# Last section of a Fourier convolution: TensorE in place of VectorE turns the blocks of the inverse, and the convolution's order is ranked anew

## The chip, the cores and the metric

The kernel runs on one core of a Trainium2 chip. The metric is the device time of one execution in microseconds (us), lower is better: the median of three runs is given, and the profile comes from one execution taken by the hardware profiler. Engines are named as in the profile: PE is TensorE (matmuls and turns), DVE is VectorE, ACT is ScalarE, POOL is GpSimd, SP issues most of the DMAs.

## The reference

One block of a sequence model on x of 2048 positions (L) by 512 channels (D), fp32. First a long convolution (a state-space kernel K made from 128 modes for each channel, applied by FFT of length 2L), then a mixer with two matmul layers and shifts along the sequence, then a two-layer MLP.

```
x = A_u
xn = layernorm(x)
K[d, l] = 2 Re sum_n C[d,n] dt[d] exp((-exp(log_A_real) + i A_imag)[d,n] dt[d] l)
y = irfft(rfft(xn, 2L) * rfft(K, 2L))[:L] + xn * D_skip
h = x + y
b = layernorm(h)
hs = shift(gelu(layernorm(b) @ w1)) @ w2      # quarters of the channels shifted by +1, -1, +2, -2
x1 = b + hs
out = h + x1 + gelu(layernorm(x1) @ w3) @ w4  # w3: 512 x 1792
```

## The kernel before

**The convolution** (`conv_phase`) works on four sections of 128 channels, numbered 0 to 3. The transform of 2048 positions is split into a part of 32 (stage A, small tables `fas`, `fis`) and a part of 64 (stage B, tables `tbs`, `ms`). The tile `h` holds the sequence as 128 partitions by 16 tiles by 512 channels. For each section:

- tables of cosines and sines in chunks of 16 channels (`table`: tiles `pt`, `cs`, `sn`, `amx`, `amp`, `E`), which ACT, DVE and POOL make together, and PE sums them to the taps `kt` (`taps`);
- stage A of the taps and of x, whose results DVE turns in blocks of 32 by 32 into `at` (`stage_a_turn`, `stage_a_x`; `stage_a_taps` for the parts that ACT copies);
- eight products e = 0 to 7 (`product`): stage B by PE (`bank<-at,tbs`), a complex product by DVE or POOL into a tile u (the names `u`, `thp`, `ini` rotate as its four homes), in part with two sums;
- the inverse of stage B (`stage_b_inv`, `bank<-u,ms`), whose 8 results ACT or DVE evict into `at`;
- DVE turns `at` in four pieces (`turn_inv`, STREAM_TRANSPOSE), and PE runs the inverse of stage A with `fis`; the result is added to `h` (`stage_a_inv`; for section 3 `last_a_inv`).

In section 3 `last_a_inv` first lays the four quarters of `h` (q = 3, 0, 1, 2: tiles 4q to 4q+3) into four banks with identity matmuls (`keep`), adds 64 small inverse matmuls to them, and ACT copies the four banks back into `h`. From the bank of q = 3 DVE also takes the statistics of tiles 12 to 15 (`part`), then means (`mvh`), and a root with one step on ACT (`ra`, `rb`, `rr`, `rn`).

**The mixer** (`mixer_phase`) begins with these tiles: `norm1(3)` normalizes tiles 12 to 15 on DVE into the first `xq` tile, `turn1(3)` turns them with 16 PE transposes into the banks `xt` (four blocks for each of the two first tiles, then the rest), ACT casts them to a high part `xt3ch` and DVE subtracts for the low part `xt3cl`, and `layer1(3, 0)` starts (`l<-xt30h,...`). From there on, matmuls of the layers follow each other to the end; the other quarters are normalized beside them.

**What sets the order.** In the convolution every step is handed to a planner (`Plan.add`) with its engine, a cost, and what it reads and writes. The planner plays the steps against these costs; where several are ready at about the same time, the table `RANK` decides. The result is one fixed order for each engine, and each engine executes its order strictly. `SHARE` says which of two engines does a shareable step. Where the planner sees PE idle it adds filler matmuls of the identity (`busy`, `bank<-ident`). In the mixer the program text is the order. PSUM has 8 banks: in the convolution two double banks (called 94 and 95 in the orders below), two single ones (96, 97), and a double one for `amx`; the mixer's `xt` banks take the space of 96, 97 and `amx`, and its other banks that of 94 and 95.

Of the kernel before, what the change touches and what calls it, by code (L numbers as in the profile page):

```python
# [1986 lines left out]
```

## Time and profile before

| what | value |
|---|---|
| median of 3 runs | 679.01 us (678.62 to 680.68) |
| profiled execution | 678.03 us |
| its span, first to last instruction | 675.8 us |
| mean granted clock of TensorE | 0.992 |
| TensorE busy | 640.8 us (95%) |
| VectorE busy | 574.7 us (85%) |
| ScalarE, GpSimd busy | 403.7 us, 398.9 us |
| start of the first layer-1 matmul | 299.83 us |

A busy TensorE includes the filler matmuls. The convolution is what runs before 299.83, the mixer what runs after it. A row of the timeline gives start, length, engine, line of the source, operation, output and inputs by name, shapes, how many instructions are merged, and, in brackets, how long the engine was idle before and who ended that. Nearly all instructions bear the line of a recording helper, so tiles tell them apart, not lines.

### The profile page before, as it was taken

The numbers are of one execution on the slowest core, as the hardware profiler recorded it, in microseconds if no ns is written. First come the engines' busy times: TensorE is split into PE (matmuls) and PEld (weight loads), VectorE is DVE, ScalarE is ACT, GpSimd is POOL, SyncE is SP. The second block draws the span as 40 slices with busy tenths as digits, with TensorE's granted clock in tenths as the row PEclk, the third lists the DMA queues.
The fourth block names the chain that finished last, engine by engine and source line by source line (L and its number), as shares of the span: only waits on it lengthen the run. The fifth ranks groups of instructions, "written<-read, shape, count | busy, mean of one in ns | idle before, by whom it ended". The sixth has DMA issues, their size and how long they took to land.

```text
span 675.8 us, 17748 instructions
## 1 busy us (share of the span) xinstructions
PE 640.8 (95%) x7232; PEld 509.2 (75%) x7232; DVE 574.7 (85%) x992; ACT 403.7 (60%) x700; POOL 398.9 (59%) x411
## 2 busy tenths in 40 slices
PE   2959999999999999999999999999999999999997
PEld 2946666773677584768888888888888889999986
DVE  5999998999899999889978799866688678888896
ACT  7998877888798883245534555544465344435430
POOL 1959798899888798502677209355511634456340
PEclk9998998999999999999999999999999999999999
DMA  8944632000301133020262524455664355434104
GB/s 201 293 134 121 206 120 48 17 3 3 81 2 50 48 114 95 2 63 1 64 202 52 167 79 156 156 179 157 195 218 140 103 162 184 129 110 141 32 0 125
DMA packets 52149, 73.58 MB, mean 109 GB/s; under 512 B 7396, under 2 KB 27108, under 8 KB 52068
## 3 DMA queue, kind: packets, MB, share of 16 engines
q1 hardware_dynamic: 50308, 69.82, 34.2%
q10 hardware_dynamic: 1248, 1.57, 0.9%
q0 software_dynamic: 512, 1.05, 0.7%
q8 instruction: 57, 0.93, 0.6%
q14 instruction: 24, 0.20, 0.1%
HBM read 44.90 MB, written 21.23 MB: 98 GB/s over the span
## 4 chain that ended last, share of the span: by engine, by line
PE 61%; DVE 4%; ACT 1%; issue 1%; DVEq 0%; ACTq 0%
PE l L140 20%; PE acc L140 7%; PE bank L140 6%; PE l3d L140 3%; PE l3a L140 3%; PE l3g L140 3%; PE l3f L140 3%; PE l3e L140 3%; PE l3c L140 3%; PE l3b L140 3%; PE res L140 2%; DVE u L140 1%; DVE at L140 1%; PE l4y L140 1%; PE l4x L140 1%; PE l4z L140 1%
## 5 line engine op out<-in xcount | busy, mean ns | idle before, releaser
L140 POOL TENSOR_TENSOR pt<-p,s 128x512 int32<-128x512 int32 x64 | 70.8, 1118 | 8.9 <-DVE sn L140 8.4
L140 ACT ACTIVATE pt<-pt 128x1056 f32<-128x1056 int32 x64 | 69.8, 1097 | 6.7 <-DVE cs L140 3.6
L140 PE MATMUL bank<-at,tbs 128*64 128x128 f32 (+1 forms) x768 | 65.5, 315 | 3.7 <-issue 1.1
L140 PEld LDWEIGHTS bank<-at,tbs 128*64 128x64 f32 x768 | 45.4, 135 | 20.3 <-issue 2.7
L140 PE MATMUL bank<-u,ms 64*128 64x128 f32 x736 | 47.6, 279 | 0.5 <-DVE u L140 0.5
L140 PEld LDWEIGHTS bank<-u,ms 64*128 64x128 f32 x736 | 43.0, 188 | 5.7 <-issue 2.0
L140 PEld LDWEIGHTS bank<-ident 128*128 128x128 f32 x310 | 37.1, 195 | 13.1 <-issue 5.3
L140 DVE TENSOR_TENSOR cs<-pt,amx 128x512 f32<-128x512 f32 x64 | 41.5, 677 | 2.1 <-ACT pt L140 1.5
L140 PE MATMUL bank<-ident 128*128 128x128 f32 x310 | 41.1, 285 | 0.7 <-DVE at L140 0.7
L140 POOL TENSOR_TENSOR cs<-pt,amp 128x512 f32<-128x512 f32 x26 | 32.5, 1252 | 9.4 <-ACT pt L140 5.4
L140 ACT ACTIVATE pt<-pt,halfpi 128x1056 f32<-128x1056 f32 x32 | 38.0, 1187 | 0.1
L140 ACT COPY at<-bank 128x512 f32<-128x512 f32 x37 | 23.1, 628 | 22.2 <-PE bank L140 22.0
L140 POOL TENSOR_TENSOR sn<-pt,amp 128x512 f32<-128x512 f32 x28 | 34.0, 1216 | 3.7 <-issue 2.0
L140 PE MATMUL bank<-cs 128*32 128x64 f32 x1024 | 32.5, 224 | 3.1 <-DVE cs L140 2.2
L140 DVE STREAM_TRANSPOSE at<-bank 128x512 f32<-128x512 f32 (+1 forms) x36 | 33.3, 953 | 1.4 <-PE bank L140 1.4
L140 PEld LDWEIGHTS bank<-cs 128*32 128x32 f32 x1024 | 23.7, 111 | 13.8 <-issue 4.6
L140 PE MATMUL bank<-sn 128*32 128x64 f32 x1024 | 31.8, 221 | 0.6 <-issue 0.5
L140 DVE TENSOR_TENSOR u<-xs,bank 128x1024 f32<-128x1024 f32 x23 | 27.9, 1217 | 3.1 <-ACT xs L140 2.7
L140 DVE TENSOR_TENSOR amx<-E,amx 128x512 f32<-128x512 f32 (+1 forms) x32 | 26.5, 829 | 3.4 <-ACT amx L140 3.3
L140 PE MATMUL bank<-h,fas 32*32 32x512 f32 x256 | 22.9, 755 | 6.8 <-ACT h L140 5.8
L140 POOL TENSOR_TENSOR cs0w<-raw,cs0w 128x512 fp32r<-128x512 f32 x5 | 6.5, 1299 | 36.7 <-ACT cs0w L140 25.5
L140 POOL TENSOR_TENSOR amp<-E,ec 128x512 f32<-128x512 f32 x23 | 24.5, 1072 | 4.1 <-DVE E L140 2.7
(1278 smaller groups left out, 2157.3 us busy)
## 6 DMA issues: line engine op xcount, KB each, us to landing
raw<-in_B_w_dram SPq DMA_DIRECT2D x28, 256.0 KB, 2.9
xq<-xq SPq DMA_DIRECT2D x72, 64.0 KB, 2.0
h<-in_A_u_dram SPq DMA_DIRECT2D x32, 128.0 KB, 4.2
h<-in_A_u_dram SPq DMA_DIRECT2D x16, 256.0 KB, 4.3
kept<-ptw SPq DMA_DIRECT2D x8, 512.0 KB, 4.4
ms<-in_mm_dram SPq DMA_DIRECT2D x4, 768.0 KB, 6.5
ptw<-kept SPq DMA_DIRECT2D x6, 512.0 KB, 4.9
out_dram<-h SPq DMA_DIRECT2D x46, 64.0 KB, 1.7
```

The lines of the kernel that those rows point to most:

```text
L140: ins = f(*args, **kw)
```

## The change

1. In section 3 (`PET = (3,)`) the inverse of stage B exchanges its operands: u is the stationary one, the table `ms` the moving one. The result comes out with channels on partitions. Its eviction into `at` writes four neighbours in a row (`128x128x4`), reading the bank with neighbours 128 or 512 elements apart; before, it read and wrote pairs.
2. The four VectorE transposes of section 3 go. Instead `turn_pe` turns eight groups of four 128 x 128 blocks on PE into a bank, and each is evicted (seven by ACT, one by DVE: `tev`). The inverse of stage A then reads its moving operand in order, with 16 matmuls of 512 columns instead of 64 of 128.
3. `last_a_back` keeps only q = 3 in a bank (one identity matmul instead of four). q = 0 and q = 2 are added to `h` by DVE; q = 1 is copied out by ACT (into the first part of `ms`) and added by POOL (`TAIL`).
4. The four normalizations of tiles 12 to 15 are planned in the convolution, write to the u tiles, which are now one tile `uu` that is also the first `xq` tile of the mixer, and the bias `rn` of the other quarters is worked out ahead of them, not behind.
5. `RANK` is new (1260 steps instead of 1252), and `SHARE` too. What VectorE does more or less by it: 2 steps of `E` fewer, 1 `amp` fewer, 1 `cs` and 2 `sn` more, 1 copy of `kt` more, 2 evictions of the far spectra (`sxv`) fewer and 1 of the near ones (`xsv`) more; the product of (section 2, e = 6) goes to POOL and that of (3, 4) comes back; of the inverse evictions (`ibv`, 7 as before) three instead of two are in section 3; of the sums section 3 has two on DVE instead of three, section 2 one as before. ACT and POOL get the rest.

Of the diff, the tables `SHARE` and `RANK` are cut:

```diff
--- before.py
+++ after.py
@@ -20,7 +20,7 @@
 EPS = 1e-5
 WID = (128, 128, 128, 128)
 CH = 16
...
 
 
 XS = 2
@@ -33,61 +33,63 @@
 LOOK = 0.05
 BS = (0, 1, 2, 3)
 FILL0 = 8.0
+PET = (3,)
+TAIL = ('dve', 'pool', 'dve')
 FILLC, FILLN = 0.3, 128
 RANK = (
-    143, 142, 183, 178, 179, 198, 203, 195, 202, 194, 189, 200, 208, 231, 207, 233, 220, 219, 196, 199, 223, 221, 225, 227,
...
+    343, 327, 391, 392, 390, 404, 399, 398, 407, 405, 402, 397, 430, 427, 456, 426, 410, 412, 403, 409, 428, 448, 436, 431,
...
 )
 TURN = 2.0 ** 32
 TWO_PI = 2.0 * math.pi
...
@@ -856,7 +860,9 @@
-    uu = [tile(f"u{i}", [128, 8 * W]) for i in range(2)]
+    cst["uu"] = tp.tile([128, 16 * W], F32, tag="uu", name="uu")
+    cst["home"] = lambda name: tp.tile([128, 16 * W], F32R, tag="uu", name=name)
+    uu = [cst["uu"][:, i * 8 * W : i * 8 * W + 8 * W] for i in range(2)]
     xs = [tile(f"xs{i}", [128, 4 * W]) for i in range(XS)]
     g_ = [t.rearrange("p (d i t) -> p d i t", i=32, t=2) for t in uu]
     uu += [t.rearrange("p g i d -> p (g i d)") for t in (thp, ini)]
@@ -985,13 +991,92 @@
                 for i, (m, t) in enumerate(terms):
                     for par in range(2):
                         f = slice(par * 64, par * 64 + 64)
+                        if s in PET:
+                            pe.matmul(plan.view(p)[:, par, pair * 128 : pair * 128 + 128], q[f, t, pair, :],
+                                      ms[f, m, e * 2 + pair, :],
+                                      start=(i == 0), stop=(i == len(terms) - 1))
+                            continue
                         pe.matmul(plan.view(p)[:, par, pair * w_ : pair * w_ + w_], ms[f, m, e * 2 + pair, :], q[f, t, pair, :],
                                   start=(i == 0), stop=(i == len(terms) - 1))
 
         p = add("PE", 0.02 + len(terms) * w_ * 4.0e-3, mm, dense=0.83, r=uk + [("mm", e // 2), ("su", s, e, 0), ("su", s, e, 1)], w=keys, bank=2)
-        dst = whole(s, 0).rearrange("p (d k t) -> p k d t", k=32, t=2)[:, e * 4 : e * 4 + 4].rearrange("p (a b) d t -> p a b d t", a=2)
-        evac("ibv", (s, e), n, 0.22 + n * 0.51e-3, dst,
-             lambda: plan.view(p)[:, :, 0 : 2 * w_].rearrange("p a (b d t) -> p a b d t", b=2, t=2), w=keys, frees=p)
+        if s in PET:
+            dst = at[:, 0].rearrange("p (i x e k) -> p e i x k", x=4, e=8, k=4)[:, e]
+            src = lambda: plan.view(p)[:, :, 0:256].rearrange("p a (b x i) -> p i x a b", b=2, x=4)
+        else:
+            dst = whole(s, 0).rearrange("p (d k t) -> p k d t", k=32, t=2)[:, e * 4 : e * 4 + 4].rearrange("p (a b) d t -> p a b d t", a=2)
+            src = lambda: plan.view(p)[:, :, 0 : 2 * w_].rearrange("p a (b d t) -> p a b d t", b=2, t=2)
+        evac("ibv", (s, e), n, 0.22 + n * 0.51e-3, dst, src, w=keys, frees=p)
+
+    def turn_pe(s, n, g, gk):
+
+        def tr():
+            for m in range(4):
+                i = n * 4 + m
+                pe.transpose(plan.view(p)[:, m * 128 : m * 128 + 128], at[:, 0, i * 128 : i * 128 + 128], ident)
+
+        p = add("PE", 0.43, tr, dense=0.0, r=[("a0", e, n) for e in RE], bank=1, w=gk)
+        evac("tev", (s, n), 512, 0.48, g, lambda: plan.view(p)[:, 0:512], w=gk, frees=p)
+
+    def stage_a_back(s, q):
+        hv = h[:, q * 4 : q * 4 + 4, OFF[s] : OFF[s + 1]]
+        u = uu[q % 2].rearrange("p (i n) -> p i n", i=2)
+        hadd = OFF[s] // 64 + q // 2 in SHARE["hadd"]
+        for i in range(2):
+            turn_pe(s, i * 4 + q, u[:, i], [("u", q % 2, i)])
+
+        def mm():
+            b = plan.view(p)
+            if hadd:
+                pe.matmul(b, ident, hv, start=True, stop=False)
+            for c in (0, 2, 1, 3):
+                pe.matmul(b[quarter(c)], fis[:, c // 2, :], u[:, c % 2], start=not hadd, stop=True)
+
+        p = add("PE", 2.24 if hadd else 1.12, mm, dense=0.76, r=[("u", q % 2, i) for i in range(2)] + ["fis", ("h", s, q)], bank=1)
+        if hadd:
+            add("ACT", 0.5, lambda: act.copy(hv, plan.view(p).rearrange("p (j d) -> p j d", j=4)), w=[("h", s, q)], frees=p)
+        else:
+            add("DVE", 0.6, lambda: v.tensor_tensor(hv, hv, plan.view(p).rearrange("p (j d) -> p j d", j=4), ALU.add),
+                w=[("h", s, q)], frees=p)
+
+    def last_a_back(s):
+
+        g = at[:, 1].rearrange("p (q i n) -> p q i n", q=4, i=2)
+        ps = {}
+        hold = lambda q: h[:, q * 4 : q * 4 + 4, OFF[s] : OFF[s + 1]]
+        view_ = lambda q: plan.view(ps[q]).rearrange("p (j d) -> p j d", j=4)
+        HK = [("h", s, r) for r in R4]
+        add("ACT", 1.5, lambda: act.activation(tiny, halfpi, AF.Sqrt), r=[("a1", q, j) for q in quads(s) for j in range(2)])
+        for q in (3, 0, 1, 2):
+            for i in range(2):
+                turn_pe(s, i * 4 + q, g[:, q, i], [("g", q, i), ("a1", q, i)])
+            if q == 3:
+                def keep():
+                    pe.matmul(plan.view(ps[3]), ident, hold(3), start=True, stop=False)
+
+                ps[3] = add("PE", 0.97, keep, dense=0.88, r=HK + [("a0", e, 0) for e in range(5)], bank=1, w=[("hq", 3)])
+            for i in range(2):
+                def mm(q=q, i=i):
+                    for c in (i, i + 2):
+                        pe.matmul(plan.view(ps[q])[quarter(c)], fis[:, c // 2, :], g[:, q, i], start=q != 3, stop=True)
+
+                n = add("PE", 0.58, mm, dense=0.73, r=[("g", q, i), "fis"], w=[("hq", q), ("last", q, i)], bank=q != 3 and i == 0)
+                ps.setdefault(q, n)
+                if i:
+                    plan.nodes[n]["spare"] = [amx.rearrange("p d i -> p (d i)")[:, 0:512]]
+            if q == 3:
+                def part():
+                    for i in range(4):
+                        v.bn_stats(bs[:, 12 + i, 1, :], plan.view(ps[3])[:, i * 128 : i * 128 + 128])
+
+                add("DVE", 0.85, part, r=[("bs", j) for j in range(12, 16)], w=[("hq", q), "part"])
+                add("ACT", 0.5, lambda: act.copy(hold(3), view_(3)), w=[("hq", 3), ("held", 3)], frees=ps[3])
+            elif TAIL[q] == "dve":
+                add("DVE", 0.6, lambda q=q: v.tensor_tensor(hold(q), hold(q), view_(q), ALU.add), r=HK, w=[("hq", q), ("held", q)], frees=ps[q])
+            else:
+                far_ = lambda q=q: ms[:, 0, 0:4, :]
+                add("ACT", 0.5, lambda q=q, far_=far_: act.copy(far_(), view_(q)), w=[("hq", q), ("held", q)], frees=ps[q])
+                add("POOL", 1.35, lambda q=q, far_=far_: gp.tensor_tensor(hold(q), hold(q), far_(), ALU.add), r=HK + [("held", q), "scaled"])
 
     def turn_inv(s, r, g, gk):
         add("DVE", 1.14, lambda: v.transpose(
@@ -1214,7 +1299,7 @@
         if not last:
             spectra_of_taps(s + 1)
             for r in range(w_ // 32):
-                stage_a_inv(s, r)
+                (stage_a_back if s in PET else stage_a_inv)(s, r)
             for r in range(WID[s + 1] // 32) if s + 1 not in FAR else ():
                 stage_a_x(s + 1, r)
         else:
@@ -1222,7 +1307,7 @@
             for i, j in enumerate(range(12, 16)):
                 add("DVE", 0.48, lambda j=j: v.bn_stats(bs[:, j, 0, :], h[:, j, 0 : OFF[s]]),
                     r=[("h", q, r) for q in range(s) for r in range(WID[q] // 32)] + [("made", s, BS[i])], w=[("bs", j)])
-            last_a_inv(s)
+            (last_a_back if s in PET else last_a_inv)(s)
 
     def finish(q, tiles=range(4)):
 
@@ -1237,7 +1322,13 @@
     add("DVE", 0.24, lambda: [op() for op in ops[:2]], r=["mv"], w=["norm"])
     add("ACT", 0.22, ops[2], w=["norm"])
     add("DVE", 0.85, lambda: [op() for op in ops[3:-1]], w=["norm"])
-    add("DVE", 0.65, lambda: None, w=["norm"])
+    x3 = cst["x3"] = [cst["uu"][:, i * 512 : i * 512 + 512] for i in range(4)]
+    for i in range(4):
+        add("DVE", 0.46, lambda i=i: v.tensor_scalar(x3[i], h[:, 12 + i, :], cst["mv"][:, 12 + i, 0:1], cst["norm"][2][:, 1, 12 + i : 13 + i], ALU.subtract, ALU.mult),
+            r=["norm", ("held", 3)], w=[("x3", i)] + [("u", i // 2, k) for k in range(2)] + ["scaled"] * (i == 3), port=True)
+    add("DVE", 0.14, ops[-1], r=["norm"])
+    add("PE", 0.44, lambda: None, r=[("x3", i) for i in range(4)] + [("last", q, i) for q in range(4) for i in range(2)], w=["turned"], dense=0.0)
+    add("ACT", 0.6, lambda: None, r=["turned"] + [("held", q) for q in range(4)])
     plan.filler = busy
     plan.run()
     return finish
@@ -1250,7 +1341,7 @@
     pool = lambda name, bufs, **kw: ctx.enter_context(tc.tile_pool(name=name, bufs=bufs, **kw))
     sl = pool("slab", 44)
     tm = pool("tm", 6)
-    w1a, w1p = pool("wrap0", 1), pool("wrap", 1)
+    w1p = pool("wrap", 1)
     sm = pool("sm", 2)
     w3p = pool("kept", 1, space=bass.MemoryType.DRAM)
     ps = pool("ps2", 4, space=PSUM)
@@ -1267,7 +1358,7 @@
     def tmp(name):
         return tm.tile([128, 512], F32, tag="g", name=name, bufs=5)
 
-    XQ = [(w1p if i else w1a).tile([128, 4 * 512], F32, tag=f"xq{i}", name=f"xq{i}") for i in range(4)]
+    XQ = [w1p.tile([128, 4 * 512], F32, tag=f"xq{i}", name=f"xq{i}") if i else cst["uu"] for i in range(4)]
     X1 = {0: XQ[3], 1: XQ[1], 2: XQ[2], 3: XQ[0]}
     quarter = lambda t, i: t[:, i * 512 : i * 512 + 512]
     turned = lambda t: t.rearrange("p (a c x) -> p c a x", a=4, c=4)
@@ -1330,13 +1421,14 @@
     H1, XL, XT = {}, {}, {}
 
     def norm1(q):
+        if q == 3:
+            XL[3] = list(cst["x3"])
+            return
         XL[q] = []
         for j in range(q * 4, q * 4 + 4):
             t = quarter(XQ[{3: 0, 0: 1, 1: 2, 2: 0}[q]], j % 4)
-            if (q < 2 and j % 2) or q == 3:
+            if q < 2 and j % 2:
                 nc.vector.tensor_scalar(t, h[:, j, :], mv[:, j, 0:1], r12[:, j : j + 1], ALU.subtract, ALU.mult)
-                if j == 15:
-                    norms(nc, cst, [3])[-1]()
             else:
                 nc.scalar.activation(t, h[:, j, :], AF.Identity, scale=r12[:, j : j + 1], bias=off12[:, j : j + 1])
             XL[q].append(t)
...
```

The order on PE at the end of section 3, before (94 to 97 are banks, `xt` those of the turned tiles):

```order
L140 MATMUL bank_94<-at,fis 32x4x32 x16
L140 MATMUL bank_96<-at,fis 32x4x32 x8
L140 MATMUL bank_97<-at,fis 32x4x32 x12
L140 MATMUL bank_96<-at,fis 32x4x32 x4
L140 MATMUL bank_95<-at,fis 32x4x32 x4
L140 MATMUL bank_97<-at,fis 32x4x32 x4
L140 MATMUL bank_96<-at,fis 32x4x32 x4
L140 MATMUL bank_95<-at,fis 32x4x32 x12
L140 MATMUL xt_0_4096<-ident,xq_4037 128x128
```

and after the change, from the third group of turns on (`bank<-ident,at` are the turns):

```order
L144 MATMUL bank_95<-ident,at 128x128 x4
L144 MATMUL bank_96<-at,fis 32x512 x4
L144 MATMUL bank_97<-ident,at 128x128 x4
L144 MATMUL bank_94<-ident,at 128x128 x4
L144 MATMUL bank_95<-ident,at 128x128 x4
L144 MATMUL bank_97<-at,fis 32x512 x4
L144 MATMUL bank_96<-at,fis 32x512 x4
L144 MATMUL bank_97<-ident,at 128x128 x4
L144 MATMUL bank_94<-ident,at 128x128 x4
L144 MATMUL bank_96<-at,fis 32x512 x4
L144 MATMUL bank_94<-ident 128x128
L144 MATMUL xt_0_4077<-ident,uu 128x128
```

All the turns and the inverse matmuls of all four quarters stand ahead of the first turn of `xt`, and bank 96 serves three quarters one after the other (q = 3, 0, 2). The first `xt` turn waited for the second of ACT's three last copies of `h` and for the first normalized tile before; now it waits for the last VectorE instruction shown in the next order, which reads bank 96.

The order on VectorE from the last inverse eviction to the normalized tiles, before:

```order
L140 COPY at<-bank_95 128x4x64x2
L140 STREAM_TRANSPOSE at<-at 128x16x2x32 x4
L140 BN_STATS bs<-bank_94 128x6 x4
L140 BN_AGGR mvh<-bs 128x2 x4
L140 TENSOR_SCALAR ra<-mvh 128x4 x2
L140 RECIPROCAL rr<-rb 128x2x4
L140 TENSOR_TENSOR rb<-rr 128x2x4
L140 SCALAR_TENSOR_TENSOR rb<-rb,ra 128x2x4
L140 SCALAR_TENSOR_TENSOR rr<-rb,rr 128x2x4
L140 TENSOR_SCALAR xq_4037<-h,mvh,rr 128x512 x4
```

and after the change:

```order
L144 BN_STATS bs<-bank_96 128x6 x4
L144 BN_AGGR mvh<-bs 128x2 x4
L144 COPY at<-bank_95 128x512
L144 TENSOR_SCALAR ra<-mvh 128x4 x2
L144 RECIPROCAL rr<-rb 128x2x4
L144 TENSOR_TENSOR rb<-rr 128x2x4
L144 SCALAR_TENSOR_TENSOR rb<-rb,ra 128x2x4
L144 SCALAR_TENSOR_TENSOR rr<-rb,rr 128x2x4
L144 TENSOR_TENSOR h<-h,bank_96 128x4x128
L144 SCALAR_TENSOR_TENSOR rn<-mvh,rr 128x2x4
L144 TENSOR_SCALAR uu<-h,mvh,rr 128x512 x4
L144 TENSOR_TENSOR h<-h,bank_96 128x4x128
```

The transposes are gone; between the means and `ra` stands the eviction of one turned group (the sixth that PE turns), ahead of the normalized tiles the add of q = 0, and behind them the add of q = 2.

More of the change, by code (lines that the diff above doesn't have):

```diff
@@ L22 @@
 CH = 16
-SHARE = {'amy': [0, 1, 2, 3, 5, 6, 7, 8, 9, 10, 11, 12, 13, 15, 17, 18, 19, 20, 22, 23, 24, 30, 31], 'csy': [2, 3, 5, 6, 8, 9, 10, 11, 12, 13, 15, 16, 17, 18, 19, 20, 21, 23, 24, 25, 26, 27, 28, 29, 30, 31], 'sny': [1, 2, 3, 4, 5, 6, 7, 8, 10, 11, 13, 14, 15, 16, 17, 18, 19, 20, 21, 22, 24, 25, 26, 27, 28, 29, 30, 31], 'sq': [0, 1, 2, 6, 8, 10, 11, 12, 13, 14, 15, 17, 18, 19, 20, 21, 22, 23, 25, 26, 29], 'nrm': [], 'nrmv': [0, 2, 11], 'ktv': [4, 7, 14, 18, 19, 21, 23], 'sxv': [(2, 5), (2, 6), (3, 3)], 'xsv': [(0, 0), (0, 2), (0, 3), (1, 3)], 'ibv': [(0, 1), (0, 3), (1, 1), (1, 6), (2, 7), (3, 2), (3, 5)], 'ev': [0, 2, 7, 8, 10, 11, 13, 15], 'pad': [('a', 0, 0, 0), ('a', 0, 1, 1), ('a', 1, 1, 0), ('a', 2, 0, 1), ('t', 0, 1, 1), ('t', 3, 0, 0), ('t', 3, 1, 0)], 'mul': [(0, 2), (1, 7), (2, 7), (3, 4)], 'turn': [1, 3, 5, 6, 7], 'hadd': [0, 1, 2], 'sumv': [(2, 6), (3, 4), (3, 6), (3, 7)], 'sump': [(0, 4), (0, 6), (1, 0), (2, 3), (2, 4), (3, 0), (3, 1), (3, 2), (3, 3), (3, 5)]}
+SHARE = {'tev': [(3, 2)], 'amy': [0, 1, 2, 3, 5, 7, 8, 9, 10, 11, 12, 13, 15, 17, 18, 19, 20, 21, 24, 26, 27, 28, 30, 31], 'csy': [2, 3, 5, 6, 8, 9, 10, 11, 12, 13, 15, 16, 17, 18, 19, 20, 21, 23, 24, 25, 26, 27, 28, 29, 30], 'sny': [1, 2, 3, 4, 5, 6, 7, 8, 10, 11, 13, 14, 15, 16, 17, 18, 20, 22, 24, 25, 26, 27, 28, 29, 30, 31], 'sq': [0, 1, 2, 6, 8, 10, 11, 12, 13, 14, 15, 17, 18, 19, 20, 21, 22, 23, 25, 26, 29], 'nrm': [], 'nrmv': [0, 2, 11], 'ktv': [7, 9, 11, 12, 14, 16, 21, 25], 'sxv': [(3, 3)], 'xsv': [(0, 0), (0, 1), (0, 2), (0, 3), (1, 1)], 'ibv': [(0, 5), (1, 1), (1, 6), (1, 7), (3, 4), (3, 6), (3, 7)], 'ev': [7, 8, 10, 12, 13, 15], 'pad': [('a', 0, 0, 0), ('a', 1, 1, 0), ('a', 1, 1, 1), ('a', 2, 0, 0), ('t', 0, 1, 1), ('t', 3, 1, 0)], 'mul': [(0, 2), (1, 7), (2, 6), (2, 7)], 'turn': [1, 3, 5, 6, 7], 'hadd': [0, 1, 2], 'sumv': [(2, 4), (3, 1), (3, 7)], 'sump': [(0, 4), (0, 6), (1, 0), (2, 3), (2, 6), (3, 0), (3, 2), (3, 3), (3, 4), (3, 5), (3, 6)]}
 XS = 2
@@ L125, in tables @@
             mm[f, 2, n, r], mm[f, 2, n, i] = -st, ct
+    if len(PET) == len(WID):
+        fi = fi.reshape(2, 2, 8, 4, 64).transpose(0, 2, 1, 3, 4).reshape(128, 2, 32).copy()
     return {"fa": fa, "fi": fi, "tb": tb, "mm": mm}
@@ L1758, in mixer_phase @@
             keep3(s + 1)
-    XH = [(w1p if i else w1a).tile([128, 4 * 512], F32R, tag=f"xq{i}", name=f"xh{i}") for i in range(4)]
+    XH = [w1p.tile([128, 4 * 512], F32R, tag=f"xq{i}", name=f"xh{i}") if i else cst["home"]("xh0") for i in range(4)]
     spare = w1p.tile([128, 512], F32R, tag="rawa", name="spare")
```

104 rows, old and new, of the table RANK are left out of this document.

## Prediction

> **What bounds the kernel now.** I read the page first, then the chain that ended last, then windows of 20 us, then groups by shape and the timeline around the end of the convolution. The first two lines of the page and six pieces of the chain (start, length, engine, tile, count):
>
> ```profile
> span 675.8 us, 17748 instructions
> PE 640.8 (95%) x7232; PEld 509.2 (75%) x7232; DVE 574.7 (85%) x992; ACT 403.7 (60%) x700; POOL 398.9 (59%) x411
> ...
> 288.83 4.74 DVE at L140 x4
> 293.61 2.82 PE bank L140 x63
> 296.45 1.14 ACT h L140 x2
> 297.63 1.46 PE xt L140 x10
> ...
> 299.83 8.75 PE l L140 x36
> ...
> 310.33 79.10 PE l L140 x348
> ```
>
> From 310.33 on the chain is matmul after matmul to the end: the mixer is bound by TensorE, and the change leaves its matmuls alone. So the time moves by what moves the first layer-1 matmul, at 299.83 now. The four rows before it are the hand-over: four VectorE transposes, the inverse transform, two copies, four turns.
>
> ```profile
> 240.00:260.00 20.00, 20.00 (x492) 16.20 (x488) 19.60 (x28) 14.05 (x25) 18.57 (x17) 1.00 0.35 97
> 260.00:280.00 20.00, 19.14 (x234) 11.35 (x220) 17.83 (x23) 4.77 (x8) 14.90 (x16) 1.00 0.20 65
> 280.00:300.00 20.00, 19.03 (x275) 14.61 (x272) 16.54 (x37) 7.19 (x13) 3.03 (x4) 1.00 0.18 54
> ```
>
> The columns are PE, PEld, DVE, ACT, POOL busy, then the granted clock. VectorE fills 19.6 of 20 us while tables are still made, and ScalarE and GpSimd are free from 260 on. So VectorE sets the pace up to the last tables, TensorE and VectorE together set it through the last section, and single dependencies set it after that. I call T0 the end of the last inverse product before the blocks are turned.
>
> **The new order ahead of T0.** The table of ranks moves almost everything a little, but the orders of the two kernels run side by side: each chunk's tables stand within a few rows of where they stood, and TensorE has 155 filler matmuls in both. What differs is who does what. VectorE's prices (and one of GpSimd):
>
> ```profile
> L140 DVE TENSOR_TENSOR u<-xs,bank 128x1024 f32<-128x1024 f32 x23 | 27.9, 1217 | 3.1 <-ACT xs L140 2.7 <-PE bank L140 0.3
> ...
> L140 DVE TENSOR_TENSOR amp<-E,ec 128x512 f32<-128x512 f32 x9 | 7.0, 774 | 0.1
> L140 DVE COPY at<-bank 128x512 f32<-128x512 f32 x7 | 4.8, 684 | 0.0
> ...
> L140 DVE TENSOR_TENSOR cs<-pt,amp 128x512 f32<-128x512 f32 x6 | 4.2, 698 | 0.0
> ...
> L140 DVE TENSOR_TENSOR E<-E 128x192 f32<-128x192 f32 x8 | 3.9, 490 | 0.0
> ...
> L140 DVE COPY xs<-bank 128x512 f32<-128x512 f32 x5 | 3.4, 689 | 2.5 <-PE bank L140 2.5
> ...
> L140 DVE TENSOR_TENSOR sn<-pt,amp 128x512 f32<-128x512 f32 x4 | 3.4, 846 | 0.0
> ...
> L140 DVE COPY kt<-bank 128x256 f32<-128x256 f32 x7 | 2.9, 417 | 0.0
> ...
> L140 DVE TENSOR_TENSOR thp<-thp 128x256 f32<-128x256 f32 x2 | 0.8, 422 | 0.0
> ...
> L140 POOL TENSOR_TENSOR cs<-pt,amp 128x512 f32<-128x512 f32 x26 | 32.5, 1252 | 9.4 <-ACT pt L140 5.4
> ```
>
> Ahead of the turns of section 2, VectorE loses two E (0.98), one amp (0.77), one spectrum eviction net (0.69), one product (1.22, now GpSimd's) and one inverse eviction (0.68); it gains one cs (0.70), two sn (1.69) and one kt (0.42). Sum: 4.34 off, 2.81 on, 1.5 us less. What it sheds goes to ScalarE and GpSimd, which have a few us in each 20. VectorE is nearly full there, so I count all of it: -1.5. Bounds: 0, if what is late next is the receiver; -4.0, if the 2.5 us of waiting at the xs copies go as well, though two of those copies stand in the new order behind the same stage-b matmuls.
>
> In section 3 VectorE gets one product more (+1.22, back from GpSimd), two sums fewer (-0.84) and one eviction more (+0.68): +1.06. TensorE's work there is the same:
>
> ```profile
> L140 PE MATMUL bank<-at,tbs 128*64 128x128 f32 x128 | 8.8, 277 | 0.4 <-DVE at L140 0.4
> ...
> L140 PE MATMUL bank<-u,fis 128*32 128x512 f32 x32 | 5.1, 710 | 0.2
> ...
> 280.43 1.22 DVE L140 TENSOR_TENSOR thp<-p,bank 128x1024 f32<-128x1024 f32 x1 [1.24 <-PE bank L140]
> ...
> 284.83 1.22 DVE L140 TENSOR_TENSOR ini<-p,bank 128x1024 f32<-128x1024 f32 x1 [0.58 <-PE bank L140]
> ```
>
> The groups are of the stretch 264.2 to 288.2, where TensorE waits for 0.6 us in two rows; VectorE waits for TensorE there (1.24 and 0.58 in the last two rows). The 1.06 more fits the waits in part. I take half as exposed, +0.5, between 0 and +1.06. The exchanged operands leave size and count of the inverse products as they were: 0, with the same VectorE waits as cover. So T0 moves by -1.0.
>
> **From T0 to the first layer-1 matmul.**
>
> ```profile
> 286.81 0.69 DVE L140 COPY at<-bank 128x512 f32<-128x512 f32 x1
> 286.99 1.16 PE L140 MATMUL bank<-ini,ms 64*128 64x128 f32 x16 [0.23 <-DVE ini L140]
> 288.19 0.61 ACT L140 COPY at<-bank 128x512 f32<-128x512 f32 x1 [1.66 <-PE bank L140]
> ...
> 294.16 0.89 DVE L140 BATCH_NORM_STATS2 bs<-bank 128x6 f32<-128x128 f32 x4 [0.60 <-PE bank L140]
> ...
> 295.41 0.24 DVE L140 TENSOR_SCALAR ra<-mvh 128x4 f32<-128x4 f32 x2
> ...
> 296.76 1.93 DVE L140 TENSOR_SCALAR xq<-h,mvh,rr 128x512 f32<-128x512 f32 x4
> 297.63 2.10 PE L140 MATMUL xt<-ident,xq 128*128 128x128 f32 x16
> 298.61 0.16 DVE L140 SCALAR_TENSOR_TENSOR rn<-mvh,rr 128x8 f32<-128x8 f32 x1
> ...
> 273.76 1.27 PE L140 MATMUL bank<-u,fis 128*32 128x512 f32 x8
> ...
> 275.13 0.66 DVE L140 TENSOR_TENSOR h<-h,bank 128x512 f32<-128x512 f32 x1
> ```
>
> Before, T0 is 286.99 + 1.16 = 288.15, and the first layer-1 matmul comes 11.7 us later. Now, with the same durations, in us after T0:
>
> - The last eviction (0.69, VectorE) ends at 0.7. Turning takes 2.10 / 16 = 0.13 for each block, 0.5 for four: first four out at 1.5.
> - ScalarE evicts at 0.61 each: the two that tiles 12 to 15 (q = 3) need end at 2.1 and 2.7. Their four inverse matmuls (1.27 for four) end at 3.6. The statistics start at 3.7, against 294.16 - 288.15 = 6.0 before. This is what the change buys: 2.3 us.
> - Statistics to root took 295.41 - 294.16 = 1.25: 4.95. But in VectorE's order one of the eight evictions stands between the means and ra. It needs the sixth block of turns, which TensorE starts only after the matmuls of q = 3: 3.6 + 12 x 0.13 = 5.2. With 0.69 it ends at 5.9. Cost: 0.95 us.
> - ra to the first normalized tile took 296.76 - 295.41 = 1.35: 7.25. But now the add of q = 0 stands ahead of them on VectorE. Its four matmuls wait for that same eviction and for ScalarE's copy of q = 3, run from 6.1 to 7.4, and then come 0.66 and rn with 0.16: 8.2. Cost: 0.95.
> - The four normalized tiles take 1.93: 10.15. ScalarE, VectorE and TensorE meanwhile bring q = 2: two more blocks of turns behind the ScalarE copy for GpSimd, two evictions, its last matmul at about 10.5. The add of q = 2 (0.66) ends at 11.2.
> - The turns of xt use banks that this last add frees: in the new order their first one waits for it, and no longer for the first normalized tile. From there 299.83 - 297.63 = 2.2 to the first layer-1 matmul: 13.4.
>
> So 13.4 against 11.7: +1.7. TensorE's 3 kept matmuls fewer and 32 turns more lie inside these waits. The four VectorE transposes that go (4.72) and the three copies of h that go from ScalarE come back as eight evictions, two adds on VectorE and one on GpSimd. That GpSimd add also stands ahead of the first split of xt on ScalarE; it starts at about 7.3, and 1.25 for such a shape (the GpSimd row above) ends it well before 11.2, so it costs nothing; the add of q = 2 covers it, and without that it would be late next. Bounds of this term: -2.3, if the chain gained all that the statistics gain, and +2.8, if every bank is late by one eviction (0.6) twice more.
>
> The chain's 36 layer-1 matmuls take 8.75, 0.243 each, against 79.10 / 348 = 0.227 after: 0.57 lost to late splits. VectorE is done earlier relative to them now, so I take back 0.2 of it (0 to 0.57). The shared home of u and the first xq tile changes no operation: 0, as the same rows stand in both orders.
>
> **Sum.** -1.5 + 0.5 + 1.7 - 0.2 = +0.5. The profiled execution took 678.03 us, 2.2 beyond its span of 675.8, so it would become 678.5. The median of the three runs is 679.01, 1.0 above it; the forecast stands against the median: 679.5.
>
> [...]
>
> **Rivals.**
>
> Faster: the re-ranking and the early statistics both hold. If the sixth eviction and the add of q = 0 cost the path nothing (0.95 each) and xt waits for the tiles alone, these end at 8.25; the first layer-1 matmul came 299.83 - 298.69 = 1.1 after them and comes at 9.4: -2.3, and with T0 at -1.5: 679.0 - 3.8 = 675.2. For it: ScalarE is idle 12.8 of 20 us there, so its evictions may come quicker. Against it: the order on VectorE is fixed, and the add of q = 2 stands behind the tiles.
>
> [...]
>
> Slower too: the new evictions read PSUM with neighbours 128 or 512 elements apart. The trace has no such read; the nearest rows are 0.61 and 0.69. If each took twice that, ScalarE's five would vanish in its idle time, VectorE's three would add up to 2.1, the last 0.7 on the path: 680.2 to 681.6. [...]
>
> No effect of the ranks, T0 unmoved and the rest as above: 680.5, inside the same case.
>
> **How the numbers follow.** A median of three runs spreads from 678.62 to 680.68, so 0.3% (2.0 us) is about what can be told from no change: 677.0 to 681.0. Forecast case (T0 between -2.5 and +0.5, hand-over +0.7 to +2.2): 0.47, 677.5 to 681. Faster rival, whole or in part, with T0 gaining up to its bound: 0.29, 674.5 to 677. Clock: 0.10; slow evictions or a later T0: 0.14, up to 683.5. The range 675.5 to 682.5 leaves about 0.1 on each side. Faster 0.29, same 0.47, slower 0.24.
>
> **What would show it.** T0 about 1 us earlier (the last inverse product's end); first statistics on the bank near T0 + 3.7; an eviction between means and ra with a wait for PE ahead of it; the first xt turn directly behind an add into h; the first l matmul 13 to 14 us after T0; evictions with four neighbours at 0.6 to 0.7; clock 1.00 through the first 5 us of layer 1. Wrong if T0 moves by over 2 us either way, which the ranks could do through ScalarE or GpSimd, whose waits I did not follow one by one, or if the hand-over is under 12 us.

## The result: 4 us slower

The changed kernel takes 681.26 us in the median of 18 runs (679.69 to 684.84), the kernel before 677.16 in as many (675.65 to 680.91). The ratio is 1.0063, 95% interval 1.0049 to 1.0078: slower by 0.6%. The forecast, 679.5, lies 1.8 under it; the time is inside the range, but the likeliest case (no change) did not come about. It went the way to which 0.24 was given.

That the time is inside the range is in part luck. The forecast was +0.5 us on a median of three runs, 679.01; in 18 runs the kernel before is 1.85 faster, at 677.16. On that median the same forecast would have read 677.7, with a range of 673.7 to 680.7, and 681.26 lies outside it: 0.5 was forecast, 4.1 was measured.

The profile after is of the slowest of the 18 runs: 684.84 us, span 682.8, mean clock 0.987. The page's first lines, and the chain of waits (start, length, engine, tile, count):

```profile
span 682.8 us, 17618 instructions
PE 645.3 (95%) x7162; PEld 510.1 (75%) x7162; DVE 573.7 (84%) x989; ACT 406.2 (59%) x705; POOL 400.9 (59%) x414
```

```profile
249.08 3.89 DMA xs<-far
...
306.08 8.52 PE l L144 x36
...
316.35 78.95 PE l L144 x348
```

A DMA stands in the chain at 249.08; the chain before had none between 236 and 262. The first layer-1 matmul starts at 306.08 instead of 299.83: 6.25 later, so in this run nearly all of the loss lies ahead of it. The hand-over, from the timeline:

```profile
291.79 1.16 PE L144 MATMUL bank<-ms,ini 64*128 64x128 f32 x16 [0.23 <-DVE ini L144]
...
296.73 0.89 DVE L144 BATCH_NORM_STATS2 bs<-bank 128x6 f32<-128x128 f32 x4 [2.98 <-PE bank L144]
...
298.24 0.69 DVE L144 COPY at<-bank 128x512 f32<-128x512 f32 x1 [0.30 <-PE bank L144]
...
300.39 0.69 DVE L144 TENSOR_TENSOR h<-h,bank 128x512 f32<-128x512 f32 x1 [0.23 <-PE bank L144]
...
301.41 1.90 DVE L144 TENSOR_SCALAR uu<-h,mvh,rr 128x512 f32<-128x512 f32 x4
...
303.23 0.67 DVE L144 TENSOR_TENSOR h<-h,bank 128x512 f32<-128x512 f32 x1
...
303.96 1.97 PE L144 MATMUL xt<-ident,uu 128*128 128x128 f32 x16 [0.40 <-DVE h L144]
...
306.08 0.73 PE L144 MATMUL l<-xt30h,cs0w 128*128 128x512 f32 x2 [0.15 <-ACT xt30h L144]
```

T0 is 291.79 + 1.16 = 292.95, which is 4.8 later than before, where 1.0 earlier was forecast. From T0 to the first layer-1 matmul it is 13.13 us against 11.68, where 13.4 was forecast. So the hand-over came out as worked out, and what had been taken for the smaller question, T0, did not.

Two places ahead of T0 differ. SP's queue around 240 us, after and then before, with VectorE's product that waits:

```profile
236.29 5.74 SPq L407 DMA_DIRECT2D xs<-far  x3
248.60 0.38 SPq L407 DMA_DIRECT2D ec<-in_B_w_dram  x1
249.08 1.36 SPq L407 DMA_DIRECT2D xs<-far  x1
...
253.07 1.22 DVE L144 TENSOR_TENSOR uu<-xs,bank 128x1024 f32<-128x1024 f32 x1 [3.47 <-DMA xs<-far]
```

```profile
234.41 8.89 SPq L403 DMA_DIRECT2D xs<-far  x4
246.49 0.32 SPq L403 DMA_DIRECT2D p<-far  x1
247.52 0.38 SPq L403 DMA_DIRECT2D ec<-in_B_w_dram  x1
```

Before, four read-backs of far spectra went out, and then a weights' load into `ec`. Now the load stands ahead of the fourth. It waited until 248.60, when the tables were done with `ec` (GpSimd's last row that reads it, `amp<-E,ec`, ends at 248.58), the read-back waited behind it, and VectorE for the read-back: 3.47 us. And TensorE's granted clock around 110 us (after, then before):

```profile
100.00:120.00 20.00, 19.39 (x376) 13.16 (x371) 14.83 (x23) 12.21 (x22) 16.62 (x16) 0.74 0.24 56
```

```profile
100.00:120.00 20.00, 18.61 (x490) 13.62 (x486) 17.32 (x28) 16.61 (x30) 17.37 (x17) 0.91 0.24 56
```

0.26 of 20 us is 5.2 us lost to half speed, against 1.8 before. In windows of 1 us the clock reads 0.50 between the two ends of the stretch, and the losses come as 5.12 and 1.71: 10.24 us at half speed from 104.9 on, against 3.42 from 108.9 on. In all twelve profiles each loss ahead of T0 is close to 1.71, 3.42 or 5.12, one, two or three times the same step; what sets the step, no run shows.

### The profile page after: what moved, and what is told of

It is laid out like the page before. It is cut to its first block, busy times and chain, and to the rows that moved or that the text cites. A ratio compares the mean times of both kernels' runs of the same rounds, so it can differ in the third digit from the quotient of the medians.

```text
span 682.8 us, 17618 instructions
## 1 busy us (share of the span) xinstructions
PE 645.3 (95%) x7162; PEld 510.1 (75%) x7162; DVE 573.7 (84%) x989; ACT 406.2 (59%) x705; POOL 400.9 (59%) x414
## 4 chain that ended last, share of the span: by engine, by line
PE 70%; DVE 15%; ACT 6%; DMA 3%; issue 3%; POOL 2%; SPq 1%; DVEq 0%; ACTq 0%; POOLq 0%
PE l L144 20%; PE bank L144 16%; PE acc L144 7%; DVE at L144 4%; ACT pt L144 3%; PE l3e L144 3%; PE l3a L144 3%; PE l3d L144 3%; PE l3c L144 3%; PE l3b L144 3%; PE l3g L144 3%; PE l3f L144 3%; DVE sn L144 3%; DVE cs L144 3%; PE res L144 2%
## 5 line engine op out<-in xcount | busy, mean ns | idle before, releaser
L144 PE MATMUL bank<-uu,ms 64*128 64x128 f32 x672 | 43.4, 279 | 1.2 <-DVE uu L144 0.8
L144 PE MATMUL bank<-ident 128*128 128x128 f32 x310 | 42.7, 291 | 1.0 <-ACT uu L144 0.5
L144 PEld LDWEIGHTS bank<-uu,ms 64*128 64x128 f32 x672 | 39.2, 188 | 5.8 <-DVE uu L144 1.9
L144 ACT COPY at<-bank 128x512 f32<-128x512 f32 x44 | 26.7, 617 | 23.7 <-PE bank L144 23.6
L144 POOL TENSOR_TENSOR cs<-pt,amp 128x512 f32<-128x512 f32 x25 | 30.7, 1227 | 9.7 <-ACT pt L144 7.5
L144 POOL TENSOR_TENSOR sn<-pt,amp 128x512 f32<-128x512 f32 x26 | 31.2, 1202 | 3.4 <-ACT pt L144 1.5
L144 DVE TENSOR_TENSOR uu<-xs,bank 128x1024 f32<-128x1024 f32 x22 | 26.7, 1216 | 4.9 <-DMA xs<-far 3.5
L144 POOL TENSOR_TENSOR amp<-E,ec 128x512 f32<-128x512 f32 x24 | 26.1, 1094 | 5.2 <-DVE sn L144 2.7
```

What stands on the lines that cost most here:

```text
L144: ins = f(*args, **kw)
```

## Experiments

The theory at the start: the hand-over costs 1.4 us as worked out, and the rest comes from the new ranks ahead of T0, by the late read-back and the clock. The rival: the exchanged inverse itself makes section 3 late.

**old_ranks_new_tail**

```diff
-SHARE, RANK = the new ones
+SHARE = before's, and 'tev'; RANK = before's for steps 0 to 1216, the new ones for the last section's tail
```

> The changed kernel's last section and hand-over, with the old ranks and shares for all steps ahead of the last inverse. Theory 1 (the loss is +1.4 us in the hand-over, and the rest comes from the new ranks ahead of T0): 1.4 us slower than before, about 678.6; T0 near 288 and the first l matmul 13.1 us after it. Theory 2 (the ranks are harmless, the exchanged inverse and its evictions make section 3 slower, and T0 late): all of the 4.3 us, about 681.4, with T0 near 291.

Measured: 679.72 us, ratio 1.0041 (1.0026 to 1.0057), about 2.8 us slower than before.

```profile
287.31 1.16 PE L144 MATMUL bank<-ms,ini 64*128 64x128 f32 x16
...
301.44 0.73 PE L144 MATMUL l<-xt30h,cs0w 128*128 128x512 f32 x2 [0.15 <-ACT xt30h L144]
```

T0 is 288.47, against 288.15 before with the same clock of 0.91 from 100 to 120, so the exchanged inverse and its evictions cost about 0.3 at most ahead of T0: the rival falls. The hand-over is 12.97. But the loss is twice the 1.4 expected, and a part of it lies behind: from the first layer-1 matmul to the end of the span it is 678.5 - 301.44 = 377.06, and before 675.8 - 299.83 = 375.97. Of that, 0.78 is one wait that the trace before does not have, of the MLP's first part for VectorE:

```profile
405.09 0.50 PE L144 MATMUL l3e<-t100h,cs1w 128*128 128x512 f32 x1 [0.78 <-DVE u L144]
```

The changed kernel has the same wait (0.78, at 409.69).

**new_ranks_old_tail**

```diff
 (the kernel before)
+SHARE = the new one without 'tev'; RANK = the new ones for steps 0 to 1216, before's behind
```

> The kernel before with the new ranks and shares for all steps ahead of the last inverse; section 3 and the hand-over as before. Theory 1: 2.9 us slower than before, about 680.0; the far spectrum of section 2 waits behind the weights' load here too (VectorE waits about 3 us for xs<-far near 250), and the hand-over is 11.7. Theory 2: no slower than before, 675.5 to 677.2.

Measured: 680.69, ratio 1.0073 (1.0046 to 1.0101), about 4 us slower. Hand-over 11.91, the rest behind it 375.95. The product at the read-back waits here too (3.10; the row names another releaser, which the SP rows explain: the load goes out at 244.25, the read-back at 244.73). By the ratios the ranks alone lose more than the tail alone, but the intervals overlap, and three of these six runs are cold (so I call runs with a mean clock of 0.991 or lower). Above 0.991 the medians are 679.4 here and 679.1 with the tail alone, against 676.6: 2.8 and 2.5. The changed kernel has 680.3 above 0.991, so the two losses do not add up; why is open.

**far_first**

```diff
+        seq.remove(1101)
+        seq.insert(seq.index(1133), 1101)   # a read-back ahead of the weights' load, in the planner's list
```

> The changed kernel with one SP instruction moved: the read-back of the last but one far spectrum of section 2 is issued ahead of the first weights' load, not behind it. If the 3.5 us in which VectorE waited for xs<-far near 250 are on the path: 2 to 3 us faster than the changed kernel, 678.3 to 679.3, and no wait for xs<-far is left over 1 us. If what follows would have waited for something else anyway (the rival): within 0.7 us of the changed kernel, 680.6 to 681.9, and another wait of 2 us or more on VectorE or TensorE between 249 and 265.

Measured: 681.34, ratio 1.0089 (1.0056 to 1.0122); VectorE still waits 3.42 for xs<-far. The edit did nothing: SP's DMAs do not follow the planner's list, as the instructions of the other engines do, but a scheduler behind it, and the order came out as in the changed kernel. So this is a second measurement of that kernel, and the sentence in the part on the kernel before that one list sets the order of each engine does not hold for SP.

**far_kept**

```diff
+    kept = lambda d, s: lambda: tc.keep_in_program_order(tc.nc.sync.dma_start(d, s))
...
-        add("SP", 0.8, dma(dst[:, 0:n], far[s, e][:, 0:n]), ...)
+        add("SP", 0.8, kept(dst[:, 0:n], far[s, e][:, 0:n]), ...)
...
-            add("SP", 0.4, dma(dst, src), ...)
+            add("SP", 0.4, kept(dst, src), ...)
```

> The changed kernel with SP's read-backs of far spectra and loads of weights held in the planner's order, which SP's own scheduler had not followed: the read-back of section 2, e = 4, now stands ahead of the first weights' load. All other engines' orders are as in the changed kernel. Theory (the wait of 3.3 to 3.5 us for xs<-far, seen in each profile with the new ranks, is the steady part of the late T0): no such wait, chunk 31 no later against before than chunk 30, and a median 2.5 to 3.2 us under the changed kernel's, 678.1 to 678.8. Rival (VectorE or GpSimd would be late there anyway): 680.5 to 681.5.

Measured: 677.87, ratio 1.0028 (1.0007 to 1.0048): 3.4 us under the changed kernel's median.

```profile
233.79 9.14 SPq L408 DMA_DIRECT2D xs<-far  x4
242.98 0.43 SPq L408 DMA_DIRECT2D ec<-in_B_w_dram  x1
...
247.16 1.22 DVE L144 TENSOR_TENSOR uu<-xs,bank 128x1024 f32<-128x1024 f32 x1
...
285.92 1.16 PE L144 MATMUL bank<-ms,ini 64*128 64x128 f32 x16 [0.23 <-DVE ini L144]
```

The four read-backs stand together again, and the product follows without a wait. Only SP's order differs from the changed kernel's, so this is the steady part of the late T0: 3.4 us by the medians, 2.4 by the two ratios to the kernel before (1.0063 and 1.0028, each beside its own runs). What is left is 1.3 us, and it is not the hand-over alone: in the profile the hand-over is 1.45 longer than before and the rest behind it 0.92, while T0 is 287.08, 1.07 earlier than before at the same clock (0.91 from 100 to 120). So with the read-back in time T0 moves by the -1.0 that was forecast; far_kept_pad below shows why.

**ranks_far_old_tail**

```diff
 (new_ranks_old_tail)
+read-backs and weights' loads kept, as in far_kept
```

> The kernel before with the new ranks and shares, the same SP order as in far_kept, and the old last section and hand-over. If the new ranks are worth the 1.5 us that VectorE sheds once the read-back is in time: T0 1 to 2 us earlier than before at the same clock, hand-over 11.7 to 11.9, and 1 us faster to equal with before in the median, 675.6 to 676.8, since cold spells of TensorE hit the new order more often. If the ranks lose elsewhere too: 678 or more.

Measured: 679.23, ratio 1.0033 (1.0005 to 1.0061). The 12 runs fall in two groups: six at a mean clock of 0.992 to 0.995 with 675.8 to 678.5 us, six at 0.984 to 0.990 with 680.0 to 684.5. Its profiled run is of the second, with 0.74 in the window 100 to 120. The expectation, equal to before or better, holds for half of the runs.

**far_kept_pad**, and with the old tail **ranks_far_old_tail_pad**

```diff
             n, c, d = pads(("a", s, r, jp), 1.12, 0.19)
+            n = 2 if (s, r, jp) == (0, 1, 1) else n   # cost, and so the order, unchanged
```

> far_kept with the two filler matmuls put back ahead of the taps' transform near 99 us (section 0, second half), which the new shares had taken away. If their absence is why TensorE's clock is at half speed from 104 to 116 in some runs with the new ranks (5.1 us lost in two of four profiles, 0 in the other two): no run at a mean clock of 0.991 or less but for one in ten, and a median 0.5 to 1.5 us under far_kept. If the spell comes from a stall of any kind at 102 to 105 (the rival): as many runs at such clocks as in far_kept, about four in ten, and a median within 0.7 us of it.

> ranks_far_old_tail with the two fillers put back: new ranks and shares, read-backs in time, old last section and hand-over. far_kept_pad's 678.8 less 1.2 (hand-over 11.9 instead of 13.1) and 0.9 (the mixer behind it 376.0 instead of 376.9): 676.7, equal to the kernel before; T0 286 to 287. If the fillers work, at most 2 of 12 runs at 0.991 or lower, where ranks_far_old_tail had 6. If they don't, 4 to 6 and a median of 678 to 679.

Measured: far_kept_pad 678.77, ratio 1.0033 (1.0013 to 1.0052), and one run of 12 at a clock of 0.991 or lower; ranks_far_old_tail_pad 677.39, ratio 1.0003 (0.9987 to 1.0020), and none of 12. With the fillers cold runs are gone (1 of 24, against 25 of 60 with the new ranks and without them), but the others cost 1 us more (677.7 to 678.8 with the new tail, 676.4 to 677.4 with the old one, this pair not run side by side, in the medians of runs above 0.991), so the median gains nothing in far_kept_pad; it gains 1.8 with the old tail, where half the runs had been cold.

That 1 us is what far_kept had gained at T0. The new `SHARE` moves fillers too, and takes these two away, which a count of 155 in both kernels does not show. With them back T0 is 286.44 at a clock of 1.00; the 288.15 of before, less the 1.71 that it lost to half speed, is 286.44 as well (an estimate from one profile each; half speed need not delay T0 in full: the profile of tail_mended, below, lost 6.83 us less ahead of T0 than that of the changed kernel, and its T0 is 5.24 earlier). So with the read-back in time and the same fillers the new ranks and shares gain nothing at T0. With the old tail the ratio is 1.0003, but of the runs of the kernel before beside it 8 of 23 are cold, and of its own none; above 0.991 it is 677.4 against 676.0, some 1.3 slower.

**before_no_pad**

```diff
 (the kernel before)
             n, c, d = pads(("a", s, r, jp), 1.12, 0.19)
+            n = 0 if (s, r, jp) == (0, 1, 1) else n
```

> The kernel before without the two filler matmuls ahead of the taps' transform near 99 us, nothing else moved. So far TensorE's mean clock was 0.991 or lower in 25 of 60 runs with the new ranks, in 1 of 12 with the new ranks and these fillers, and in 9 of 46 runs of the kernel before. If the fillers make that difference: some 4 to 6 of 12 runs at 0.991 or lower, these 2 us or more slower than the rest. If it is the new order around 100 to 104 us: 1 to 3 of 12 as before, and a median within 0.5 us of before.

Measured: 675.09, ratio 0.9977 (0.9959 to 0.9996): faster, with one run of 12 at 0.991 or lower, where the kernel before had 8 of 23 beside it. So missing fillers alone do not make cold runs; whether there are fewer without them in the old order, 12 runs are too few to say (of all 69 runs of the kernel before, 17 were cold).

```profile
100.00:120.00 20.00, 19.05 (x480) 14.04 (x482) 19.45 (x32) 18.27 (x33) 18.06 (x17) 1.00 0.23 52
...
283.50 1.16 PE L140 MATMUL bank<-ini,ms 64*128 64x128 f32 x16 [0.23 <-DVE ini L140]
```

T0 is 284.66 in its profile, 3.5 earlier than in that of before, which lost 1.7 to half speed. Above 0.991 the medians are 675.0 and 676.0: for the third time the two fillers cost 1.0 us in runs that are not cold. This is the one version that beats both kernels.

**tail_mended**

```diff
-SHARE = {'tev': [(3, 2)], ...
+SHARE = {'tev': [], ...
+    for n, p in {1246: 0, 1231: 1, 1227: 2, 1229: 3}.items():
+        plan.nodes[n]["home"] = p              # inverse of q = 2 and q = 0 in banks 94 and 95
+    for n in (1233, 1248):
+        plan.nodes[n]["deps"].update(range(1253, 1257))   # both adds behind the four tiles
...
-    norm1(3), finish(0, early), turn1(3), gelus(), finish(0, late), ...
+    norm1(3), turn1(3), gelus(), finish(0, early), finish(0, late), ...
```

> The changed kernel with VectorE relieved in the hand-over: the eviction between means and ra goes to ScalarE, both adds into h stand behind the four normalized tiles, their quarters lie in banks 94 and 95 so that xt waits for neither, and the statistics of other tiles stand behind the splits of xt. If VectorE's chain sets the hand-over, as predicted (0.95 + 0.95 + the add behind the tiles): the first l matmul 10.8 to 11.3 us after T0 instead of 13.1, the time 2 us shorter than the changed kernel, about 679.2. If TensorE itself is the bound there (its turns and inverse matmuls follow each other with under 0.7 us of gaps from 293.85 to 303.1): 12.2 to 12.6 after T0, and 0.5 to 0.9 us shorter, about 680.5.

Measured: 684.7, ratio 1.0114 (1.0082 to 1.0146), with four of six runs cold. Its profiled run was not: T0 287.71, hand-over 12.97. That is 0.16 under the changed kernel, and old_ranks_new_tail has 12.97 without any relief, so it bought nothing. But VectorE was hardly relieved. Its first normalized tile starts 6.97 after T0, in the changed kernel 8.46, but its last ends at 10.05, in the changed kernel 10.36: between them the small step `rn`, 0.16 long before, takes 1.24 and ends when GpSimd's add of q = 1 ends, at 296.4.

```profile
294.96 1.40 POOL L144 TENSOR_TENSOR h<-h,ms 128x512 f32<-128x512 f32 x1 [9.91 <-ACT ms L144]
295.14 1.24 DVE L144 SCALAR_TENSOR_TENSOR rn<-mvh,rr 128x8 f32<-128x8 f32 x1
```

In the same place the rows of TensorE follow each other, and end later still, at 298.56:

```profile
288.61 1.49 PE L144 MATMUL bank<-ident,at 128*128 128x128 f32 x12
...
290.03 1.41 PE L144 MATMUL bank<-at,fis 128*32 128x512 f32 x8
...
291.37 1.53 PE L144 MATMUL bank<-ident,at 128*128 128x128 f32 x12
...
296.34 1.80 PE L144 MATMUL bank<-at,fis 128*32 128x512 f32 x8
...
298.07 0.49 PE L144 MATMUL bank<-ident 128*128 128x128 f32 x2
...
298.62 1.97 PE L144 MATMUL xt<-ident,uu 128*128 128x128 f32 x16
```

The mixer behind it took 678.7 - 300.68 = 378.0, 1.1 more than in far_kept (376.89). TensorE waits there for 1.3 us in three rows, in far_kept for 0.9 in two; that the statistics put off to behind the splits cause this was not tested.

**light_turns**

```diff
 (tail_mended)
-            for m in range(4):
+            for m in range(4 if n % 4 == 3 else 1):
```

> tail_mended with 18 of the 32 turns of section 3 left out (three of the four blocks in each of six groups), so that TensorE has about 2.3 us less to do in the hand-over, with the same evictions, waits and VectorE order. If TensorE's own work is the bound there: the first l matmul 11.0 to 11.6 us after T0 instead of 12.97. If the chain over VectorE and ScalarE is: 12.5 or more.

Measured in one run: T0 288.94, first layer-1 matmul at 300.92, hand-over 11.98, between the two expectations. With 2.3 us of TensorE's work gone the hand-over loses 1.0, no more, since VectorE's tiles end only just ahead:

```profile
297.19 1.45 DVE L144 TENSOR_SCALAR uu<-h,mvh,rr 128x512 f32<-128x512 f32 x3
...
298.86 1.97 PE L144 MATMUL xt<-ident,uu 128*128 128x128 f32 x16
```

So two chains of almost the same length lead to `xt`: VectorE's from the statistics to the tiles, and TensorE's turn, ScalarE's eviction, TensorE's matmul, quarter after quarter. With VectorE's steps moved the hand-over is 0.16 shorter than in the changed kernel, with TensorE lightened as well 1.15; TensorE lightened alone was not run, and `rn` takes 1.24 here too.

All profiles but that of light_turns together, in us (clock: granted in the window 100 to 120; rest: from the first layer-1 matmul to the end of the span). Elsewhere ahead of T0 the clocks are alike but in two: tail_mended lost 1.7 us less to half speed from 40 to 60 (0.91 against 0.83), far_first 1.7 more from 240 to 280.

| kernel | ranks | read-back | clock | T0 | hand-over | rest |
|---|---|---|---|---|---|---|
| before | old | in time | 0.91 | 288.15 | 11.68 | 375.97 |
| before_no_pad | old | in time | 1.00 | 284.66 | 11.71 | 375.93 |
| old_ranks_new_tail | old | in time | 0.91 | 288.47 | 12.97 | 377.06 |
| after | new | late | 0.74 | 292.95 | 13.13 | 376.72 |
| far_first (as after) | new | late | 0.74 | 295.11 | 13.13 | 376.36 |
| tail_mended | new | late | 1.00 | 287.71 | 12.97 | 378.02 |
| new_ranks_old_tail | new | late | 1.00 | 289.54 | 11.91 | 375.95 |
| far_kept | new | in time | 0.91 | 287.08 | 13.13 | 376.89 |
| far_kept_pad | new | in time | 1.00 | 286.44 | 13.13 | 377.23 |
| ranks_far_old_tail | new | in time | 0.74 | 290.00 | 11.91 | 375.99 |
| ranks_far_old_tail_pad | new | in time | 1.00 | 287.70 | 11.93 | 375.97 |

## Where the prediction held and where it missed, step by step

- **T0, -1.0: the step that failed.** In the medians it is some 2 us later: of the 4.1 us between 681.26 and 677.16, the hand-over has 1.4 and the rest of the mixer 0.8. In the profile it is 4.8 later, well over the 2 us that the prediction itself gave as a sign of being wrong. Two things were missed. I followed the orders of the four engines and left SP's out, where a load that had stood behind a read-back now stands ahead of it. That costs 2.4 to 3.4 us (far_kept). And the -1.5 for what VectorE sheds was taken whole, where 0 was its bound. far_kept does show T0 1.07 earlier, but with the two fillers back nothing of that is left: had the number come true, it would have been by TensorE's fillers, not by VectorE's load. The trace before had VectorE at 19.6 of 20 us from 240 to 260, but at 17.5 from 180 to 200, with TensorE at 19.8 (row below), and the first was read as if it held all the way. GpSimd, said to be free from 260 on, is busy for 14.90 of 20 us in the row that the prediction shows (260 to 280); only ScalarE is free. The +0.5 for section 3 can't be told apart in these runs.
- **The clock.** 0.10 was given to a time made longer by the clock, with 1.00 through the first 5 us of layer 1 as the test. No run shows what that chance rests on: after the turns of `xt` the clock stayed at 1.00 (each 2 us from 300 to 314, profile after). It falls at 104.9 us instead, in a part that the prediction didn't look at, and costs 5.12 us in that profile. Cold runs (mean clock of 0.991 or lower) were 25 of 60 with the new ranks and 17 of 69 of the kernel before, a difference that could be chance or not; with the runs above 0.991 alone the changed kernel is at 680.3 in the median and the kernel before at 676.0 to 676.6 (its runs beside the experiments), so the loss is there without it.
- **The hand-over, +1.7: right in size**, 13.13 against 13.4: statistics 3.78 after T0 (3.7), the eviction ahead of ra, an add ahead of the tiles, one behind them, `xt` behind that add. **Half right in its cause:** the text gave VectorE's eviction and adds the blame; moving them gave 0.16. TensorE's own turns fill the same time, and `rn` on VectorE, 0.16 before, takes 0.49 in the changed kernel and 1.24 in tail_mended, both times ending within 0.02 us of GpSimd's add, which was put at nothing. Of the quarters, the add ahead of the tiles is that of q = 2 and the one behind that of q = 0; the texts had them the other way round, and nothing in the sum hangs on it. "3 kept matmuls fewer and 32 turns more lie inside these waits" was the weak sentence: there were hardly any waits.
- **Early layer 1, -0.2: right there** (8.52 for the 36 matmuls, before 8.75), but the new tail brings 0.4 to 1.3 more behind it, most of it the 0.78 at the MLP's first part.
- **Evictions with four neighbours: right.** 0.59 on ScalarE, 0.69 on VectorE (before 0.61 and 0.69; rows below). That rival is out, and so is the faster one: its 9.4 us for the hand-over is reached by none of the profiles.
- **Turns on TensorE at 0.13 us: right.** In the rows of tail_mended above 24 turns take 1.49 + 1.53 us, 0.13 each, as the trace before had it (2.10 for sixteen). The rows for the evictions, of the profile after:

```profile
290.77 0.59 ACT L144 COPY at<-bank 128x512 f32<-128x512 f32 x1 [3.71 <-PE bank L144]
...
293.06 0.69 DVE L144 COPY at<-bank 128x512 f32<-128x512 f32 x1 [0.76 <-PE bank L144]
```

The row for 180 to 200 us, of the profile before:

```profile
180.00:200.00 20.00, 19.80 (x402) 15.37 (x400) 17.49 (x27) 17.13 (x29) 16.96 (x17) 1.00 0.06 17
```

What stays open is why an order is prone to cold runs. In the new order they went when two fillers came (1 of 24); in the old order there were few without the fillers (1 of 12), which may be chance. In the new order a stall of TensorE is gone with the fillers: 16 matmuls of `kt` and `fas`, 1.09 us in a row in the profile before, run from 101.20 to 103.93 in the changed kernel, and TensorE is busy for 0.39 of the us from 102 to 103; in far_kept_pad and ranks_far_old_tail_pad it is busy for all of it. Of the seven profiles with the new ranks and without the fillers, four have it busy for 0.39 or less there (the changed kernel, far_first, far_kept, ranks_far_old_tail) and lose 1.7 to 5.1 us to half speed behind it; three have 0.74 to 0.86 (light_turns, new_ranks_old_tail, tail_mended) and lose nothing between 100 and 120. That the stall brings the fall is a guess from these nine profiles, and why its length differs from profile to profile is open.

## What to carry to other kernels

When an order is ranked anew, compare the DMA queues as closely as the engines: here one load that had to wait held up the read-back behind it, and a row such as `[3.47 <-DMA xs<-far]` shows up only afterwards. Compare fillers by place and not by number, since two of them cost 1 us here. Before moving work from a busy engine to TensorE, look whether TensorE has gaps in that very place: in this hand-over it had hardly any, so count its rows from the first dependency to the last before taking its time as covered. And where single runs spread by 5 us, split them by their clock before reading a profile, since one profile is one draw.

## What was unexpected in the hardware

In the profile of far_first a small add on VectorE took 4.75 us, where the same instruction took 0.51 in tail_mended. VectorE's row, then GpSimd's:

```profile
99.02 4.75 DVE L144 TENSOR_TENSOR kt<-kt,dsk 128x16 f32<-128x16 f32 x1
```

```profile
98.23 1.29 POOL L144 TENSOR_TENSOR sn<-pt,amp 128x512 f32<-128x512 f32 x1
99.44 1.11 POOL L144 TENSOR_TENSOR pt<-p,s 128x512 int32<-128x512 int32 x1
100.46 1.11 POOL L144 TENSOR_TENSOR amp<-E,ec 128x512 f32<-128x512 f32 x1
101.49 1.11 POOL L144 TENSOR_TENSOR pt<-p,s 128x512 int32<-128x512 int32 x1
102.51 1.21 POOL L144 TENSOR_TENSOR cs<-pt,amp 128x512 f32<-128x512 f32 x1
```

It ends at 103.77, just when the fourth of the GpSimd instructions that follow each other from 99.44 on ends (103.72). That GpSimd's instructions held it up is a guess from the equal ends. So long an add was seen in one profile of twelve; there TensorE stood still for 3.57 us behind it and the clock fell, but it fell as far (0.74) in two profiles without such a stall. The same holds of `rn` in the hand-over: 1.24 in tail_mended, ending at 296.38 where GpSimd's add ends at 296.36, and 0.49 in the changed kernel, ending at 301.48 and 301.46. No run moved GpSimd's instructions away to test it.
